# TensorE's order in the attention stage: values one head pair later, half blocks turned first

## The chip, the cores and the metric

The kernel runs on one core of a Trainium2 chip. The metric is the device time of one execution in microseconds (us). TensorE multiplies matrices and turns blocks, VectorE, ScalarE and GpSimd do the elementwise work, SyncE's queue starts most transfers. The core has SBUF as working memory and PSUM, eight banks of 128 x 512 fp32, as the place to which TensorE writes.

## The reference: causal attention, then a routed expert layer

```python
def _attn_ref(q, k, v):                      # batch 4, 12 heads, 448 tokens, head size 64
    scores = scale * np.matmul(q, k.transpose(0, 1, 3, 2))
    scores = np.where(mask, -1000000000.0, scores)      # mask: above the diagonal
    scores = scores - np.max(scores, axis=-1, keepdims=True)
    attn = np.exp(scores)
    attn = attn / (np.sum(attn, axis=-1, keepdims=True) + 1e-09)
    return np.matmul(attn, v)

def _moe_ref(x, w_gate, w1, w2):             # 1792 tokens of 768, 8 experts of 1024
    cap = N // E
    logits = x @ w_gate
    # all (token, expert) pairs in falling order of logit; a token goes to the first
    # expert that still has room for it (cap tokens each)
    ...
    for e in range(E):
        mask = assigned == e
        out[mask] = np.maximum(x[mask] @ w1[e], 0.0) @ w2[e]
```

The attention's output, heads side by side, is the `x` of the expert layer. Everything is fp32.

## The kernel before: a planned list of work for each engine

The 48 heads are taken as 24 head pairs (`NP`), six pairs to a batch. For one pair, with its two heads as sides 0 and 1, the attention stage does this.

- **Scores** (`scores`, L225): query blocks of 128 tokens against the keys that the causal mask leaves, blocks of 192, 320, 448 and 64 keys (`QM`). Two steps of two blocks each, (2, 3) and then (1, 0). The operands use 64 of the array's rows, one half for each side. The results go to PSUM tiles `s`, four buffers.
- **Masks** on VectorE (`mask`, L237): the mask is added, the maximum taken, the result lies in `Sm`. **Exponentials** on ScalarE (`exp`, L247) write the block of probabilities `P` (tile name `P`, two buffers) and the row sums `rs`.
- **Transposes** (`transp`, L257): 16 blocks of 128 x 128 are turned into PSUM tiles `t`, in four groups of four. Groups 0 and 1 are the whole blocks of side 0 and 1, group 2 more whole blocks of both sides, group 3 the half blocks of both sides.
- **Copies** of the turned groups (`keep_pt`, L280) into one of two tiles `PT`: group 0 and 1 on ScalarE (128 x 512 each), group 2 and the two halves of group 3 (64 x 256 each, numbers 3 and 4) on ScalarE or VectorE.
- **Values** (`av`, L292): `V` against `PT`, accumulated in one tile `t`; side 0 fills the array's first 64 columns, side 1 the others. The key block 0 comes first and needs the copies 0, 1, 3 and 4, the blocks 1 to 3 need copy 2. The result is copied to `xt` (L306), on ScalarE or VectorE.
- **Rows** (`rows_at`, L527; pairs 0 to 11 only): `xt` is turned back (L324) into a tile `t`, and VectorE divides by the row sums while it copies (L348). Pairs 12 to 23 are turned later, while the routing runs.
- **Logits** (`logits`, L542, and `logits_back`, L559): for sets of four pairs, `xt` against the gate weights (L359), a copy `lt`, four transposes (L378) and VectorE's sums (L398 to L407). The last two pairs go another way (L368).

All tiles `t` take turns in four PSUM buffers, in the order in which TensorE's steps are written out, so a step waits until the tile that stands four before its own has been read.

The order of the work comes from two places. TensorE's steps form one chain: `pe` (L454) makes every step depend on the step before, so TensorE does them as `plan` (L414) lists them, in its loop over `n`. The work of the other engines is put in order by `Schedule.run` (L123) before the kernel is built: it knows a duration for each task (the numbers in `add` calls), takes the earliest engine that has ready work, and there the task of the highest priority. The priority falls with the number of the pair (`pr = 5.5 - 0.1 * pp`), copies get 0.3 more, masks 0.25. The result is a fixed order of instructions for each engine; on the chip each engine works through its own, and semaphores do the waiting.

After attention come the routing rounds (class `Router`) and eight experts (class `Experts`), whose weights are loaded as the routing names each expert. They have a plan of their own that begins when attention ends.

Of the kernel before, what the change touches and what calls it, by code (L numbers as in the profile page):

```python
# [74 lines left out]
class Schedule:  # L75
# [7 lines left out]
    def add(self, eng, dur, fn, deps=(), prio=5.0, lat=None, delay=0.0, mode=0):  # L83
        t = Task(eng, dur, fn, prio, lat, delay, mode)
        for d in deps:
            if d is None:
                continue
            if d.end is None:
                d.users.append(t)
                t.wait += 1  # L90
            else:
                self.after(t, d)
        if not t.wait:
            self.put(t)
        return t
# [65 lines left out]
class Attention(Schedule):  # L161
# [252 lines left out]
    def plan(self, rt):  # L414
        add = self.add
        self.rings = {}
        self.got, self.gotv, self.vfree, self.qfree = {}, {}, {}, {}
        self.exps, self.pts, self.rec, self.xts, self.log, self.done_x = {}, {}, {}, {}, {}, []
        self.line = self.last_ev = None
        got, gotv = self.got, self.gotv  # L420
        prev = None
        for g in range(NP // 2):
            free = []
            if g >= 4:
                free = [self.event(0.0) for _ in range(2)]
                self.qfree[2 * g - 7], self.vfree[2 * g - 7] = free
            if g == 0:
                self.half0 = add("DMA", 0.7, self.load0, [], 9.5, 3.4)
            for p0, w in ((0, 1), (1, 1)) if g == 0 else ((2 * g, 2),):
                prev = add("DMA", 1.1 * w, lambda p0=p0, w=w: self.load(p0, w), [prev] + free, 9.0, 2.2 if prev else 3.8)  # L430
                for u in range(w):
                    got[p0 + u] = prev
            prev = gotv[g] = add("DMA", 1.1, lambda g=g: self.load_v(g), [prev] + free, 9.0, 2.2)
        for n in range(NP + 3):
            for lst in ((2, 3), (1, 0)):
                self.score_set(n, lst)
            self.turns(n - 1)
            self.rows_at(n - 3)
            self.logits_back(n - 3)
            self.values(n - 1)  # L440
            self.logits(n - 2)
        more = self.extras(rt)
        prev = None
        b3 = [self.log[b] for b in range(B - 1)]
        for n, early in more:
            prev = add("DVE", 0.3, n, [prev or self.exps[1, 1, 1]] + (b3 if early else []), 2.0)
        self.run()
# [36 lines left out]
    def turns(self, pp):  # L484
        if not 0 <= pp < NP:
            return
        pr = 5.5 - 0.1 * pp
        every = [(sd, i) for sd in range(2) for i in range(NC)]
        for g, need in ((0, [(0, 0), (0, 1), (0, 2)]), (1, [(1, 0), (1, 1), (1, 2)]), (3, every),
                        (2, [(0, 1), (0, 2), (1, 1), (1, 2)])):  # L490
            a = self.pe(0.44, lambda g=g: self.transp(pp, g), [self.exps[pp, sd, i] for sd, i in need] + self.ring("t", 4))
            last = [a]
            for c in (3, 4) if g == 3 else (g,):
                dur = {"DVE": 0.61, "ACT": 0.49} if c < 3 else {"DVE": 0.35, "ACT": 0.27}
                one = c < 2
                last = [self.add("ACT" if one else "ACT/DVE", dur["ACT"] if one else dur,
                                 lambda e="ACT", c=c: self.keep_pt(e, pp, c), last + self.ring("av", 2), pr + 0.3)]
                self.pts[pp, c] = last[0]
            self.rings.setdefault("t", []).append(last)

# [832 lines left out]
```

## Time and profile before

| | |
|---|---|
| median of 3 runs | 503.51 us (502.6 to 508.95) |
| profiled execution | 505.04 us, span of its instructions 503.3 us |
| attention stage in the profile | 0 to about 183 us, 24 head pairs |
| busy in the span | TensorE 487.1, its weight loads 409.2, VectorE 383.5, ScalarE 298.3, GpSimd 53.2 us |
| clock that TensorE was granted | 1.00 of full speed in the windows of the attention stage |

The span runs from the first instruction to the last of one execution; the time of the execution lies 1.74 us above it. Times of rows are counted from the start of the span. In the rows, PE is TensorE's matmuls, PEld its weight loads (which run ahead beside matmuls), DVE is VectorE, ACT ScalarE, POOL GpSimd. A row `t<-PT,v` is an instruction that writes tile `t` from `PT` and `v`. TensorE's fp32 matmuls appear as two records each, so a step of eight matmuls shows sixteen.

### The profile page before, as it was taken

The page shows a single profiled execution, that of the slowest core. Times are in us where ns is not written, and L with a number is a line of the kernel's source. Part 1 is how long each engine was busy: PE and PEld are TensorE (multiplying, and loading weights), DVE is VectorE, ACT ScalarE, POOL GpSimd, SP SyncE. Part 2 cuts the span into 40 slices and gives each one's busy share as a digit, 9 for nine tenths or more (in the row PEclk, how much of TensorE's full clock was granted, in tenths as well). Part 3 has the DMA queues.
Part 4 walks back from the last instruction along what each step waited for, and adds up shares of the span by engine and source line. Part 5 has one row for each costly group of instructions (what it writes and reads, how often), then busy time and mean ns, then how long its engine had stood idle before and what let it go on. Part 6 is the DMA issues. An engine that isn't in the chain of part 4 may idle for free.

```text
span 503.3 us, 10215 instructions
## 1 busy us (share of the span) xinstructions
PE 487.1 (97%) x3697; PEld 409.2 (81%) x3697; DVE 383.5 (76%) x1326; ACT 298.3 (59%) x749; POOL 53.2 (11%) x100
## 2 busy tenths in 40 slices
PE   8999999999999999899999999999999999999995
PEld 4676767766665676799998999989989999999994
DVE  4778878886776976589999999999999686594410
ACT  4887768777776853235655556645364574664410
POOL 6000000000000011010130120110022310210101
PEclk9999999999999999999999999999999999999999
DMA  8633183135000007748856876783793986682101
GB/s 280 265 109 112 44 294 120 43 115 191 37 0 1 3 31 238 267 158 327 257 185 188 295 221 211 223 265 124 234 314 99 322 278 229 190 288 73 56 1 55
DMA packets 19187, 84.84 MB, mean 169 GB/s; under 512 B 2240, under 2 KB 4928, under 8 KB 19136
## 3 DMA queue, kind: packets, MB, share of 16 engines
q1 hardware_dynamic: 16464, 73.14, 43.4%
q0 software_dynamic: 2672, 11.04, 6.9%
q8 instruction: 29, 0.48, 0.4%
q14 instruction: 22, 0.18, 0.1%
HBM read 73.16 MB, written 11.01 MB: 167 GB/s over the span
## 4 chain that ended last, share of the span: by engine, by line
PE 67%; DVE 16%; ACT 8%; DMA 5%; issue 3%; POOL 0%; POOLq 0%; DVEq 0%; ACTq 0%
PE po L1258 18%; PE t L297 11%; PE ph L1224 9%; PE s L233 8%; DVE wl L1154 5%; PE t L268 5%; PE ph L1228 4%; ACT P L254 4%; DMA xio<-xd,idx 4%; ACT PT L272 3%; PE ph L1219 3%; DVE G L697 2%; PE rt L798 1%; DVE Sm L244 1%; PE po L1219 1%
## 5 line engine op out<-in xcount | busy, mean ns | idle before, releaser
L1154 DVE TENSOR_TENSOR wl<-wr,wh 128x512 fp32r<-128x512 f32 x180 | 116.3, 685 | 14.2 <-ACT wh L1148 13.9
L1148 ACT CAST wh<-wr 128x1536 fp32r<-128x1536 f32 x60 | 88.9, 1481 | 60.7 <-DMA wr<-in_w 41.2
L254 ACT ACTIVATE P<-Sm,mx 128x448 f32<-128x448 f32 (+2 forms) x192 | 95.8, 500 | 39.7 <-DVE mx L244 39.3
L1224 PE MATMUL ph<-xhl,wh 128*128 128x448 f32 x336 | 109.2, 380 | 0.0
L1228 PE MATMUL ph<-xhl,wl 128*128 128x224 f32 x336 | 88.8, 264 | 0.0
L1258 PE MATMUL po<-wh,HH 128*112 128x384 f32 x256 | 68.2, 342 | 0.0
L1258 PE MATMUL po<-wh,HL 128*112 128x384 f32 x256 | 67.9, 341 | 0.0
L1258 PE MATMUL po<-wl,HH 128*112 128x384 f32 x256 | 67.3, 339 | 0.0
L1224 PEld LDWEIGHTS ph<-xhl,wh 128*128 128x128 f32 x336 | 63.1, 188 | 5.1 <-issue 0.6
L297 PE MATMUL t<-PT,v 128*64 128x192 f32 (+3 forms) x384 | 62.7, 387 | 3.4 <-ACT PT L272 2.5
L1228 PEld LDWEIGHTS ph<-xhl,wl 128*128 128x128 f32 x336 | 64.1, 191 | 0.0
L297 PEld LDWEIGHTS t<-PT,v 128*64 128x64 f32 x384 | 36.4, 136 | 31.1 <-ACT PT L272 15.8
L233 PE MATMUL s<-raw 64*128 64x448 f32 (+3 forms) x384 | 52.2, 406 | 0.3 <-DVE mx L244 0.2
L233 PEld LDWEIGHTS s<-raw 64*128 64x128 f32 x384 | 31.9, 188 | 19.4 <-issue 13.3
L268 PE MATMUL t<-idf,P 128*128 128x128 f32 x384 | 47.4, 276 | 0.0
L268 PEld LDWEIGHTS t<-idf,P 128*128 128x128 f32 x384 | 41.5, 140 | 6.1 <-issue 5.2
L1258 PEld LDWEIGHTS po<-wl,HH 128*112 128x112 f32 x256 | 44.0, 174 | 0.3
L1258 PEld LDWEIGHTS po<-wh,HL 128*112 128x112 f32 x256 | 43.2, 175 | 0.2
L1258 PEld LDWEIGHTS po<-wh,HH 128*112 128x112 f32 x256 | 43.1, 175 | 0.3
L244 DVE CUSTOM_DVE_ANT_0 Sm<-s,MK 128x448 f32<-128x448 f32 (+2 forms) x72 | 33.5, 486 | 11.3 <-PE s L233 10.8
L244 DVE CUSTOM_DVE_ANT_0 Sm<-s,MR 128x64 f32<-128x64 f32 (+3 forms) x120 | 40.1, 379 | 0.1
L1234 ACT ACTIVATE HH<-hs 128x224 fp32r<-128x224 f32 x56 | 21.9, 391 | 26.3 <-DVE hs L1242 24.5
(170 smaller groups left out, 625.8 us busy)
## 6 DMA issues: line engine op xcount, KB each, us to landing
wr<-in_w SPq DMA_DIRECT2D x64, 768.0 KB, 5.5
raw<-in_qk SPq DMA_DIRECT2D x11, 896.0 KB, 8.7
v<-in_v SPq DMA_DIRECT2D x12, 512.0 KB, 3.7
xd<-xio SPq DMA_DIRECT2D x2, 1152.0 KB
xd<-xio SPq DMA_DIRECT2D x3, 576.0 KB, 3.6
xd<-xio SPq DMA_DIRECT2D x3, 192.0 KB, 3.2
raw<-in_qk SPq DMA_DIRECT2D x1, 448.0 KB, 4.3
xd<-xio SPq DMA_DIRECT2D x1, 384.0 KB, 3.9
```

What stands on the lines that cost most here:

```text
L233: self.nc.tensor.matmul(ts[sd][:, o:o + m], q[:, 0, QS[i]:QS[i] + P], k, start=True, stop=True)
L244: self.nc.vector.tensor_tensor_reduce(Sm[:, QO[i] + sd * m:QO[i] + sd * m + m], self.S.pop((pp, sd, i)), mk, -0.125, 3.0e38, OP.add, OP.mi ...
L254: self.nc.scalar.activation(X[:, s], Sm[:, s], AF.Exp, bias=mx[:, sd, i:i + 1], scale=-1.0, accum_out=self.RS[b][:, pr, sd * NC + i:sd * N ...
L268: self.nc.tensor.transpose(t[:, n * P:n * P + P], X[:, o:o + P], idf)
L297: self.nc.tensor.matmul(self.AV[pp][sd * 64:sd * 64 + 64, XO[j]:XO[j] + KM[j]], self.V[2 * pp + sd][:, j, :], self.PTs[pp % 2][:, sd, KO[j ...
L1148: self.nc.scalar.copy(hi, self.R[p, c])
L1154: self.nc.vector.tensor_sub(lo[:, s], self.R[p, c][:, s], hi[:, s].bitcast(F32))
L1219: nc.tensor.matmul(t[:, c], self.R[p, f // 2][:, s], self.X[0, 0][:, d, 0, c], start=d == 0, stop=d == 5)
L1224: nc.tensor.matmul(t[:, :2 * CAP], hi[:, s], x[:, d].rearrange("p z t -> p (z t)"), start=d == 0, stop=False)
L1228: nc.tensor.matmul(t[:, :CAP], lo[:, s], x[:, d, 0], start=False, stop=d == 5)
L1234: self.nc.scalar.activation(self.HH[p][:, f], self.P[p, f][:, :CAP], AF.Relu)
L1258: self.nc.tensor.matmul(self.T[p, "o", u][z][:, :384], a[p][:, f, u * C:u * C + C], w[:, o:o + 384], start=f == 0 and n == 0, stop=f == 7 ...
```

## The change

In the loop of `plan` the call for values moves from behind the logits' transposes to ahead of the pair's transposes, and takes the pair before. For turn `n` TensorE's order was: scores of pair n, transposes of n-1, rows of n-3, logits' transposes, values of n-1, logits. It becomes: scores of n, values of n-2, transposes of n-1, rows of n-3, logits' transposes, logits.

In `turns` group 3, the half blocks, becomes the first of the four groups, ahead of 0, 1 and 2. Every group now waits for all eight exponentials of its pair; before, groups 0 and 1 waited for three of their own side, group 2 for four. The copies of group 3's two halves get 0.6 more priority instead of 0.3.

```diff
         for n in range(NP + 3):
             for lst in ((2, 3), (1, 0)):
                 self.score_set(n, lst)
+            self.values(n - 2)
             self.turns(n - 1)
             self.rows_at(n - 3)
             self.logits_back(n - 3)
-            self.values(n - 1)
             self.logits(n - 2)
...
-        for g, need in ((0, [(0, 0), (0, 1), (0, 2)]), (1, [(1, 0), (1, 1), (1, 2)]), (3, every),
-                        (2, [(0, 1), (0, 2), (1, 1), (1, 2)])):
+        for g, need in ((3, every), (0, every), (1, every), (2, every)):
...
+                up = 0.6 if c > 2 else 0.3
                 last = [self.add("ACT" if one else "ACT/DVE", dur["ACT"] if one else dur,
-                                 lambda e="ACT", c=c: self.keep_pt(e, pp, c), last + self.ring("av", 2), pr + 0.3)]
+                                 lambda e="ACT", c=c: self.keep_pt(e, pp, c), last + self.ring("av", 2), pr + up)]
```

## Rows read from the trace of the kernel before

**Rows 1.** The page: busy shares; costliest groups (busy, mean ns, idle before, releaser).
```profile
PE 487.1 (97%) x3697; PEld 409.2 (81%) x3697; DVE 383.5 (76%) x1326; ACT 298.3 (59%) x749; POOL 53.2 (11%) x100
...
L297 PEld LDWEIGHTS t<-PT,v 128*64 128x64 f32 x384 | 36.4, 136 | 31.1 <-ACT PT L272 15.8
```

**Rows 2.** Windows: length, then busy of PE, PEld, DVE, ACT, POOL.
```profile
20.00:30.00 10.00, 9.79 (x77) 7.32 (x76) 8.47 (x42) 9.43 (x33) 0.00 (x0) 1.00 0.48 159
...
51.18:80.55 29.37, 29.00 (x223) 20.21 (x222) 23.48 (x94) 22.30 (x77) 0.30 (x2) 1.00 0.42 146
...
139.31:168.67 29.36, 28.46 (x207) 18.98 (x206) 21.64 (x94) 22.41 (x78) 0.00 (x0) 1.00 0.00 1
```

**Rows 3.** Chain of waits, turns with rows: start us, us, engine, tile, line.
```profile
23.25 2.04 PE s L233 x16
...
27.62 2.31 PE t L297 x14
...
58.30 2.04 PE s L233 x16
60.34 1.90 PE t L268 x16
62.24 0.44 PE t L324 x4
62.67 2.75 PE t L297 x13
```

**Rows 4.** Chain of waits, a turn without rows.
```profile
146.43 1.17 PE s L233 x8
...
149.43 1.07 ACT PT L272 x2
...
151.60 1.94 PE t L297 x11
153.55 1.17 PE s L233 x8
```

**Rows 5.** Timeline, one turn: start us, us, engine, line, operation [idle before, releaser].
```profile
59.45 0.62 DVE L244 CUSTOM_DVE_ANT_0 Sm<-s,MK 128x448 f32<-128x448 f32 x1 [0.16 <-PE s L233]
...
61.24 0.35 DVE L244 CUSTOM_DVE_ANT_0 Sm<-s,MK 128x192 f32<-128x192 f32 x1
61.30 1.07 ACT L272 COPY PT<-t 128x512 f32<-128x512 f32 x2
...
62.26 0.68 ACT L254 ACTIVATE P<-Sm,mx 128x448 f32<-128x448 f32 x1
62.60 0.19 PEld L297 LDWEIGHTS t<-PT,v 128*64 128x64 f32 x2 [0.17 <-ACT PT L272]
...
63.05 0.37 ACT L272 COPY PT<-t 64x256 f32<-64x256 f32 x1
...
63.47 1.81 PEld L297 LDWEIGHTS t<-PT,v 128*64 128x64 f32 x14 [0.68 <-ACT PT L272]
...
65.45 0.62 DVE L274 COPY xt<-t 128x448 f32<-128x448 f32 x1 [1.21 <-PE t L297]
```

**Rows 6.** Chain of waits: a logits step, and the end of the attention stage.
```profile
72.53 0.89 PE t L359 x8
...
168.67 2.04 PE s L233 x16
...
172.72 2.69 PE t L297 x13
175.41 0.88 PE t L359 x4
176.29 1.90 PE t L268 x16
...
178.57 2.08 PE t L297 x14
```

**Rows 7.** Chain of waits: values of pair 1, ahead of scores of pair 3.
```profile
20.87 2.38 PE t L297 x14
```

## The prediction

> **What bounds the kernel now.** The first view is the page's busy shares [rows 1]: TensorE is busy for 97% of the span. That reading would leave nothing to win, so the second view asks how true it is by stage. In the attention stage TensorE counts 29.00 of 29.37 us as busy, its weight loads only 20.21, and VectorE and ScalarE 22 to 23 [rows 2]: no engine is plainly full. The Trainium skill, "Perfetto Trace Analysis", section Identifying the Most-Contended Engine, says that a tensor engine's matmul busy share is no measure of its limit and that the share of weight loads is a better one. The trace agrees (97% against 81%), and by the matmul share alone the sum below would be zero.
>
> The third view is the chain of waits. From 52 us on, a turn with rows reads: scores 2.04, transposes of the pair 1.90, row transposes 0.44, values 2.75 [rows 3], each behind the last, so TensorE's own order is the chain. But values needs only 1.94 once its operands are there [rows 4]. The missing 0.81 is seen in the fourth view, the timeline [rows 5]: of the 16 weight loads of a values step two start at 62.60 and fourteen at 63.47, after 0.68 us of waiting for ScalarE's copy of a half block into PT. That copy could not start before 63.05, because ScalarE had first done two whole-block copies (61.30, 1.07 us) and an exponential (62.26, 0.68 us) that stood ahead of it. Values of pair n comes straight after the transposes of pair n, with only 0.44 us of other work between, so the five copies are exposed on TensorE. In the second half, where no row transposes stand between, the chain leaves TensorE for ScalarE's copies on its way from scores to values, and a turn takes 7.12 us (153.55 minus 146.43) [rows 4] for 2.04 + 1.90 + 1.94 = 5.88 us of matmul work.
>
> **The change, step by step.** The program's order on TensorE is strict (each step depends on the one before), so the new order will be there.
>
> Step 1, values of a pair moved one turn later. Between scores of pair 3 (23.25) and scores of pair 23 (168.67) lie 20 turns and 145.42 us [rows 3, 6]. Their matmul work, from pieces of the chain that wait for nothing: 20 x (2.04 + 1.90 + 1.94) = 117.6; row transposes in 12 turns x 0.44 = 5.3; five logits steps x 0.89 = 4.5; five times their four transposes, as long as the rows', x 0.44 = 2.2 [rows 3, 4, 6]. Together 129.5, so 15.9 us (0.80 a turn) is waiting for copies. After the change, row transposes or nothing, then the scores of the next pair (2.04 us) stand between the last transpose and values. A turn with rows, counted from its scores: scores to 2.04, values to 4.0, transposes to 5.9, rows to 6.3, values of the turned pair at 8.4. The copies (two of 0.53, one of about 0.6, two halves of about 0.4) have 2.5 us against the 1.2 that they need now. I remove the whole 15.9.
>
> Step 2, what is late next. PSUM tiles t rotate over four buffers. The new order in them is values, group 3, 0, 1, 2, rows. Counted back four, group 2 takes the buffer of values of the same turn, so it waits for that tile's eviction. Three groups (12 transposes of about 0.11, some 1.4 us) cover VectorE's 0.62 us copy and its start [rows 5]. That leaves about 0.5 us, and a mask of 0.62 us in progress eats it. Likewise the row step waits for the two half-block copies, which is why being turned first helps them. ScalarE has 5.6 us of work a pair and VectorE 5.4 to 5.9 (two windows of four pairs each [rows 2]) against turns of 5.9 to 6.7: 85 to 95% full, in program order, so some waits will come back. Bounds: 0 a turn (scores and transposes in the chain of rows 3 lose nothing today) and 0.37 (what values loses in the early turns, 2.31 minus 1.94, with ScalarE 94% busy [rows 2, 3]). I take 0.15, nearer the lower end since only group 2's wait has a cover under one VectorE instruction: 20 x 0.15 = +3.
>
> Step 3, transposes all wait for every exponential of their pair. Group 3 is first and needs them all. Transposes of a pair now start 1.94 us later after the scores of the next pair than before, so this wait has more cover, not less. Zero; it would cost up to the last two exponentials, about 0.9, if ScalarE fell behind by more than 1.9 us.
>
> Step 4, changes of array shape. A turn has three before and three after, but scores to values, values to transposes and transposes to scores are new. Nearest rows: the narrow logits step costs 0.88 ahead of transposes and 0.89 ahead of scores, and transposes behind it take the usual 1.90 [rows 6]. The first weight load of values is idle for 0.17 behind the row transposes [rows 5], the only such gap that a row gives. Three new switches at up to 0.17 make 0.5; I take zero, with half of that, 0.25 a turn (5 us), either way as the bound.
>
> Step 5, both ends. In front, scores of pair 3 stand ahead of values of pair 1 instead of behind them: up to 2.4 us earlier [rows 7], or nothing if ScalarE's exponentials hold the transposes. At the back one values step (1.94) more follows the last scores, less the 0.75 that values of pair 22 waits now (2.69 minus 1.94) [rows 6], which the logits step then mostly covers. Net -1, bounds -3 and +2. Loads, row stores and routing constants: loads of v are freed a turn later, which is covered by their being issued seven pairs ahead; no queue is passed otherwise. The routing work of VectorE that starts after pair 19's logits keeps its order, and everything behind the last values (from 180.6 us) follows attention's end.
>
> Sum: -15.9 + 3 - 1 = -13.9 us. The profiled execution took 505.04 (span 503.3), so 491.1; it lies 1.5 above the median, 503.51, which gives 489.6. I forecast **490**, 2.7% less.
>
> **Rivals.**
> A second case, *the queues of ScalarE and VectorE bind*: the early turns show it, 6.68 us a turn with ScalarE at 9.43 of 10 [rows 2, 3]. All 20 turns at that pace would be 12 x 6.68 + 8 x 6.24 + 6.7 for logits = 136.8, so 8.6 saved and 1 at the ends: 494. Against it: in those turns values still stood right behind its copies. Chance 0.19.
>
> A third, *the copies stay late*: ScalarE does them behind all exponentials of the next pair. From a turn's start the first scores are there at 1.2 [rows 4] and the first mask at 1.9; the exponentials, ScalarE's 5.6 us less 1.4 of copies [rows 2, 5], take 4.2 and would end near 6.1 if nothing held them and near 7.6 as paced today, and copies behind them near 9.0, against the 8.4 at which values wants them: 0.6 lost a turn instead of 0.8, so 500 to 503. The Trainium skill, "PSUM — Partial Sum Buffer", section Engine vs sequencer instructions, calls ScalarE's queue a strict FIFO; the trace agrees, with the half copy at 63.05 behind the exponential of 62.26. Against this rival: copies of the older pair are given the higher priority, and the whole-block ones go promptly today. Chance 0.07.
>
> On the other side, *the eviction of values holds up group 2*. Today VectorE is idle for 1.21 us when values ends, and copies at once [rows 5]. In the new order values ends while masks of the newest pair run. If the copy stands behind a whole run of them (six from 59.45 to 61.59, 2.15 us [rows 5]), group 2 is late by 2.15 - 0.5 = 1.65 a turn, 33 us, and against the 16.9 saved that is 520, slower. It decides from 1.85 us of queueing a turn. Against it: the older pair's copy has the higher priority, so it should stand behind one mask. Chance 0.06.
>
> **How the numbers follow.** My case has 0.68: 485 to 493.4 with the bounds of steps 2, 4 and 5, its low end being all waits gone (503.5 - 15.9 - 3 = 484.6). Two per cent, about what a measurement of this kernel tells from no change, is 10 us, so 493.4. Faster: 0.68 and a little of the second case, 0.70. Within 2%: the rest of the second and the third, 0.24. Slower: 0.06. The range 484.5 to 500 takes in my case and the second, about 0.86.
>
> **What would show it.** Right: chain turns near 6.3 to 6.5 us with rows and 5.9 to 6.1 without; values at 1.94 to 2.0 with its weight loads started together; the idle time of its weight loads behind ScalarE's copies (15.8 us now [rows 1]) near zero; the last values ending near 167 instead of 180.7 us [rows 6]; the rest the same length. Wrong: the last four transposes of a pair waiting for the copy of values (the last rival), values waiting for PT as now (the third), scores or transposes longer than 2.04 and 1.90 without a wait (step 4), or the routing stage giving the gain back.

## The result, and the profile after

The median fell from 503.08 us (502.6 to 508.95, four runs; the forecast stood on the first three, 503.51) to **487.88 us** (485.98 to 492.33, four runs): a ratio of 0.9681, interval 0.9595 to 0.9766. The forecast was 490. The profiled execution took 486.56 us, its span 484.9, so the span is 18.4 us shorter than before. All of that lies in the attention stage of the two profiles. The last values step ends at 162.10 us instead of 180.66 [rows 6], 18.56 us earlier, and what follows it takes 322.8 us, against 322.64 before (503.3 minus 180.66).

The page first, busy shares and then the group of values' weight loads, which answers to [rows 1]:

```profile
PE 471.2 (97%) x3697; PEld 398.3 (82%) x3697; DVE 376.7 (78%) x1316; ACT 298.9 (62%) x759; POOL 52.6 (11%) x100
...
L297 PEld LDWEIGHTS t<-PT,v 128*64 128x64 f32 x384 | 25.4, 136 | 23.8 <-issue 14.0
```

TensorE's share is 97% as before, so this row alone would show no change. The second does: most of the idle time ahead of values' weight loads now ends with "issue" (14.0 of 23.8 us), where the engine waits for nothing that the profile shows. ScalarE's copies, 15.8 us of it before, no longer lead the list. Two windows of four pairs each, with the columns of [rows 2], show it by stage:

```profile
52.57:78.91 26.34, 26.34 (x223) 18.69 (x222) 22.05 (x94) 22.81 (x79) 0.30 (x2) 1.00 0.46 161
117.33:141.92 24.59, 24.59 (x206) 16.93 (x206) 20.42 (x88) 22.44 (x79) 0.00 (x0) 1.00 0.02 5
```

The same instructions of TensorE as in [rows 2] (223 matmul records in the first window) took 29.37 us and take 26.34, with no idle time left in either window. The chain of waits, a turn with rows, one without, and the end of the stage:

```profile
52.57 2.04 PE s L233 x16
54.61 1.88 PE t L297 x16
56.49 1.90 PE t L268 x16
58.39 0.44 PE t L324 x4
58.82 2.04 PE s L233 x16
...
129.40 2.04 PE s L233 x16
131.44 1.88 PE t L297 x16
133.32 1.90 PE t L268 x16
135.21 2.04 PE s L233 x16
...
148.17 2.04 PE s L233 x16
...
160.20 1.90 PE t L297 x16
```

From 25.35 us on the chain lies on TensorE alone. A turn with rows is 6.25 us (58.82 minus 52.57), one without 5.81 (135.21 minus 129.40), against 7.12 for both kinds before [rows 3, 4]. Values is 1.88 with all sixteen records in one piece; before, in the turns with rows from 52 us on, it was 2.75 with its weight loads split [rows 3, 5].

### The profile page after: what moved, and what is told of

It is laid out like the page before. It is cut to its first block, busy times and chain, and to the rows that moved or that the text cites. A ratio compares the mean times of both kernels' runs of the same rounds, so it can differ in the third digit from the quotient of the medians.

```text
span 484.9 us, 10216 instructions
## 1 busy us (share of the span) xinstructions
PE 471.2 (97%) x3697; PEld 398.3 (82%) x3697; DVE 376.7 (78%) x1316; ACT 298.9 (62%) x759; POOL 52.6 (11%) x100
## 4 chain that ended last, share of the span: by engine, by line
PE 77%; DVE 11%; ACT 5%; DMA 4%; issue 2%; POOL 1%; POOLq 0%; DVEq 0%; ACTq 0%
PE po L1258 23%; PE ph L1224 10%; PE s L233 9%; PE t L297 9%; PE t L268 8%; PE ph L1228 5%; DVE wl L1154 4%; PE ph L1219 3%; ACT P L254 3%; DMA xio<-xd,idx 2%; DVE G L697 2%; PE ph L1189 2%; PE rt L798 2%; DMA out<-xio,idx 1%; PE po L1219 1%
## 5 line engine op out<-in xcount | busy, mean ns | idle before, releaser
L297 PE MATMUL t<-PT,v 128*64 128x448 f32 (+3 forms) x384 | 46.8, 386 | 0.0
L297 PEld LDWEIGHTS t<-PT,v 128*64 128x64 f32 x384 | 25.4, 136 | 23.8 <-issue 14.0
L274 DVE COPY PT<-t 64x256 f32<-64x256 f32 (+1 forms) x56 | 29.6, 529 | 16.3 <-PE t L268 10.5
```

The lines of the kernel that those rows point to most:

```text
L274: self.nc.vector.tensor_copy(out, x)
L297: self.nc.tensor.matmul(self.AV[pp][sd * 64:sd * 64 + 64, XO[j]:XO[j] + KM[j]], self.V[2 * pp + sd][:, j, :], self.PTs[pp % 2][:, sd, KO[j ...
```

## The experiments

Each ratio is against runs of the kernel before on the same chip. An experiment is the kernel before or the changed kernel with one edit; the diff shows the edit, and `...` stands for lines left out.

### The order alone, the half blocks not first, as before

The changed kernel, with the groups in the order of before, 0, 1, 3, 2, and the old priority of the copies.

```diff
-        for g, need in ((3, every), (0, every), (1, every), (2, every)):
+        for g, need in ((0, [(0, 0), (0, 1), (0, 2)]), (1, [(1, 0), (1, 1), (1, 2)]), (3, every),
+                        (2, [(0, 1), (0, 2), (1, 1), (1, 2)])):
...
-                up = 0.6 if c > 2 else 0.3
```

> The new order of TensorE's steps with the groups of transposes as before (0, 1, 3, 2, each waiting for its own exponentials). Theory D (the turn by which values moved is the whole gain): the same as the changed kernel, 485 to 490 us, and values' weight loads wait for no copy of ScalarE. Rival H (the half blocks turned first bring part of it): the half copies come later again, 0.2 to 0.4 us lost in each of 20 turns, 491 to 496 us.

Measured: 489.07 us, ratio 0.9676 [0.9635, 0.9718]. The chain of waits:

```profile
53.54 2.04 PE s L233 x16
55.58 1.88 PE t L297 x16
57.46 1.90 PE t L268 x16
59.35 0.50 PE t L324 x4
59.86 2.04 PE s L233 x16
```

The turn is 6.32 us and the last values ends at 163.37, which is 1.27 us behind the full change. The order of TensorE's steps carries the whole gain as far as the times can tell: the two ratios are 0.0005 apart.

### The half blocks first alone, in the order of before

The kernel before, with group 3 first and the new priority of its copies.

```diff
-        for g, need in ((0, [(0, 0), (0, 1), (0, 2)]), (1, [(1, 0), (1, 1), (1, 2)]), (3, every),
-                        (2, [(0, 1), (0, 2), (1, 1), (1, 2)])):
+        for g, need in ((3, every), (0, every), (1, every), (2, every)):
...
+                up = 0.6 if c > 2 else 0.3
```

> The old order of TensorE's steps with the half blocks turned first. Theory D: the half copies get ahead of the exponential, but the copies of the whole blocks, 1.07 us of ScalarE, still stand between the last transposes and values: about half of the 0.8 us a turn stays, 494 to 499 us. Rival H: most of the gain, 486 to 491 us.

Measured: 507.96 us, ratio 1.0035 [1.0000, 1.0071]; the last values ends at 182.66, later than before. Both theories expected a gain, and there is none. The weight loads of values still wait for ScalarE's copies (14.2 us, 40 times). The chain of one turn:

```profile
111.19 1.17 PE s L233 x8
112.36 0.60 DVE Sm L244
...
113.07 1.75 ACT P L254 x6
...
114.84 0.37 ACT PT L272
...
115.24 0.59 ACT PT L272
...
115.87 2.43 PE t L297 x14
118.31 1.17 PE s L233 x8
```

The last copy to come is now that of a whole block (0.59 us) instead of a half block, and the turn is 7.12 us as before. So which copy comes last is not the point. The chain shows a **loop**, work that runs from one engine to the next and back to its start: the first half of the newest scores, its mask, the first exponentials of that pair, and only then, in ScalarE's fixed order, the older pair's remaining copies; then values, and behind values the next scores. The chain of [rows 4] has the same start and end. In these turns values waits for the copies that ScalarE does after those exponentials, and the next scores wait for values.

### Four more transposes ahead of values, in the kernel before and in the one after

Both kernels write four identity transposes into the tile that values then overwrites, 24 times. This is extra work on TensorE and nothing else.

```diff
             self.AV[pp] = self.ps.tile([P, 512], F32, name="t", bufs=4)
+            for i in range(4):
+                self.nc.tensor.transpose(self.AV[pp][:, i * P:i * P + P], self.k["idf"], self.k["idf"])
```

> The kernel before with four more transposes (of the identity, into the tile that values then overwrites) ahead of each values step: 24 x 0.44 = 10.5 us more work of TensorE, waiting for no copy. Theory D: values is waiting in that time anyway, so 503 to 506 us. Rival F (the values step is long for a reason on TensorE itself, and its whole share is work): 513 us or more.

> The changed kernel with the same four more transposes ahead of each values step. Theory D: TensorE has no waiting left in which to hide them, so all of it shows, 10.5 us and up to 3.5 more for an array shape that now changes four times a turn: 497 to 502 us. Rival Q (VectorE or ScalarE now set the pace and TensorE has slack): less than 5 us more, under 493 us.

Measured: on the kernel before 509.69 us, ratio 1.0086 [1.0053, 1.0119], between the 503 to 506 of theory D and the 513 of its rival; on the kernel after 499.41, ratio 0.9895 [0.9863, 0.9927], which is 0.0214 above the change, or 10.8 us. The chains of the kernel before with the extra work, and of the kernel after with it:

```profile
118.35 2.04 PE s L233 x16
120.39 1.90 PE t L268 x16
122.28 0.44 PE t L296 x4
122.72 2.75 PE t L299 x13
125.47 2.04 PE s L233 x16
```

```profile
56.07 2.04 PE s L233 x16
58.10 0.59 PE t L296 x4
58.69 1.88 PE t L299 x16
60.57 1.90 PE t L268 x16
62.47 0.44 PE t L326 x4
62.91 2.04 PE s L233 x16
```

In the kernel before the turn stays 7.12 us with 0.44 us more in it: the extra work sits in the wait. The first turns show the same, 6.68 us with the extra work (36.13 minus 29.45 in that profile's chain) and without it (36.61 minus 29.93), although the loop is shorter there. The last values ends only 1.68 us later, at 182.34, for 10.6 us of added work. The two profiled executions differ by 5.3 us (510.34 and 505.04). The rest of that lies behind the attention stage (326.3 us against 322.64), where nothing was changed; over the profiles of this document in which that part is the same code it takes from 321.9 to 326.35 us. In the kernel after every turn pays in full: 6.84 instead of 6.25 us, and the last values ends at 175.90, 13.8 us later (24 x 0.575). TensorE had no slack left. The time shows less than the profile, 10.8 us by the ratios, and the profiled execution was the slowest of the five (501.51).

This is also where a rule and the trace part. In the window from 52.57 us of the changed kernel, weight loads fill 18.69 of 26.34 us, 71%. The Trainium skill, "Perfetto Trace Analysis", section Identifying the Most-Contended Engine, would judge TensorE's headroom by that share, and by the share of its peak arithmetic that the kernel uses, rather than by its matmuls' 100%. Before the change the share of weight loads was 69% (20.21 of 29.37 us [rows 2]) and there was room indeed, although about 10% and not 31%. After it the share is nearly the same, and added work found no room. So here the matmul share tells whether more work fits into this order of steps, and the share of weight loads does not.

### The eviction of values behind the other work

This builds the rival on the other side: the copy of values' tile gets less priority than everything of the newer pair that stands in its way.

```diff
-        self.xts[pp] = self.add("ACT/DVE", {"ACT": 0.475, "DVE": 0.56}, ev, [a, self.xts.get(pp - 1)], pr + 0.3)
+        self.xts[pp] = self.add("ACT/DVE", {"ACT": 0.475, "DVE": 0.56}, ev, [a, self.xts.get(pp - 1)], pr - 0.6)
```

> The changed kernel with the copy of values' result (xt) at a lower priority, so that it stands behind all masks of the newest pair in VectorE's order. Theory E (the prediction's last rival, made on purpose: group 2 of the transposes waits for that copy and has about 0.5 us of cover): the copy starts some 0.4 to 1.0 us after values ends, 0.3 to 0.8 lost a turn, 493 to 504 us. Rival: the cover is ample, 486 to 490 us.

Measured: 493.52 us, ratio 0.9788 [0.9769, 0.9808], so 5.4 us of the gain are lost by the ratios. The edit moved more than a place in the order: in this trace 22 of the 23 whole copies of values run on VectorE, where the changed kernel has 4 there and 19 on ScalarE. The 5.4 us are the price of both together. Waits of the transposes' weight loads, from 20 to 170 us, and then the timeline around one of them (start, us, engine, line, operation, idle before and releaser):

```profile
PEld t L268 <- ACT PT L272: 5.7, 8, 1.2
```

```profile
80.43 1.04 ACT L272 COPY PT<-t 128x512 f32<-128x512 f32 x2
...
80.93 0.62 DVE L274 COPY xt<-t 128x448 f32<-128x448 f32 x1
...
81.05 0.66 PE L268 MATMUL t<-idf,P 128*128 128x128 f32 x4 [0.49 <-ACT PT L272]
```

The cost was in the range expected (493 to 504), the mechanism was not as expected. The last four transposes start at 81.05, before values' copy ends at 81.55 (80.93 + 0.62). They start as the first of ScalarE's two copies ends, about 80.95 (80.43 plus half of 1.04). So they did not take the buffer of values; by the time, they took that of group 0 of the same pair, whose copy stands behind the newest pair's exponentials. My text ahead of the result, four tiles counted back, does not hold at this place. The buffers are fixed when the program is built, so this is a fact of the program and not of the chip; no run shows how they were given out.

### Values one turn late, but behind the transposes

```diff
-            self.values(n - 2)
             self.turns(n - 1)
+            self.values(n - 2)
```

> The changed kernel with values of the older pair behind the transposes instead of ahead of them (scores n, transposes n-1, values n-2, rows). Theory D (only the turn's delay counts, not the place in the turn): 486 to 491 us. Rival P (the place counts: transposes come 1.9 us earlier and now wait for exponentials): 0.3 or more lost a turn, over 494 us.

Measured: 496.42 us, ratio 0.9833 [0.9805, 0.9860]. The time was in the range of the rival theory, but mostly not for its reason. Waits of weight loads from 20 to 170 us:

```profile
PEld t L297 <- ACT PT L272: 5.4, 17, 0.4
...
PEld t L268 <- ACT P L254: 0.9, 2, 0.7
```

The transposes hardly wait for exponentials. Values' weight loads do wait, although their own operands were copied a turn earlier. The timeline of ScalarE's copies in one turn, and the chain of the next, whose values step reads them:

```profile
58.28 1.47 ACT L272 COPY PT<-t 64x256 f32<-64x256 f32 x3
```

```profile
61.24 1.17 PE s L233 x8
...
63.12 1.75 ACT P L254 x6
...
64.89 0.38 ACT PT L272
...
65.31 1.95 PE t L297 x16
67.26 0.59 PE t L324 x4
```

ScalarE had done its copies for this values step by 59.75 (58.28 + 1.47), and VectorE the last one by 59.49. Yet values starts at 65.31, right behind a copy of the *newer* pair (64.89 + 0.38). It reads nothing of that copy, so what it waits for should be a PSUM tile; this is inferred, as the trace does not name the buffers. Behind four transpose groups all four buffers `t` are taken, and here the first to be emptied waits for a copy that stands behind the exponentials again. The loop is half closed through the buffers.

This wait is not the whole loss, and not every wait of a weight load delays TensorE. From scores of pair 3 (20.67) to scores of pair 23 (156.29) the stage takes 135.6 us, 6.9 more than with the change. By the starts in the timeline, values that begin late make about 3.3 us of this. A row step takes 0.59 us behind values and 0.44 behind transposes, 1.8 us in twelve turns. The five logits steps take about 2.1 us more, now that they stand close behind the values whose copy they read. Values ahead of the transposes, as the change has it, is therefore worth having, 7.7 us by the ratios, but the wait for buffers is only about half of the reason.

### ScalarE's order alone

TensorE's order is that of before; ScalarE must do the copies 0, 1, 3 and 4 of a pair ahead of the next pair's exponentials.

```diff
                 self.pts[pp, c] = last[0]
+                for sd, i in every if c != 2 and pp + 1 < NP else ():
+                    last[0].users.append(self.exps[pp + 1, sd, i])
+                    self.exps[pp + 1, sd, i].wait += 1
```

> The kernel before, in its old order on TensorE, with ScalarE's and VectorE's order planned so that the exponentials of the next pair come behind the copies of a pair's turned blocks 0, 1, 3 and 4. Theory L (a loop: scores, masks, exponentials, copies, values, scores; no order of ScalarE alone opens it, since copies 2.0 and exponentials 4.0 then stand in line between one pair's transposes and the next, 6.9 a turn): 497 to 503 us. Rival O (the whole loss was a bad order of ScalarE's queue): 486 to 493 us.

Measured: 498.05 us, ratio 0.9873 [0.9837, 0.9909]. The last values ends at 170.45, so the attention stage gained 10.2 us; 326.35 us behind it took part of that back. The chain, a turn without rows:

```profile
109.57 2.04 PE s L233 x16
111.61 0.60 PE t L268 x4
...
112.29 0.40 ACT PT L272
...
113.26 0.37 ACT PT L272
...
113.67 2.41 PE t L297 x14
116.08 2.04 PE s L233 x16
```

The turn is 6.51 us. The exponentials are out of the chain, so the loop through them is shown to be what made 7.12. The time is in the range of theory L, but that theory had said 6.9 a turn and that no order of ScalarE would open the loop. A turn with rows takes 6.51 too (61.89 minus 55.38 in the same profile's chain), so a shorter loop is left: values still stands 1.9 us behind the start of its transposes, and the copies themselves are exposed. Reordering ScalarE's queue takes the exponentials out of the loop; of the versions tried, only moving values puts other matmuls over the copies.

### A further step: more row transposes in the turns

The rows of six more pairs, 18 instead of 12, are turned in the attention stage. That loads the full TensorE there and leaves six pairs for the routing, in two pieces fewer.

```diff
-LATE = 12
-PIECES = {14: 3, 17: 3, 20: 3, 22: 2, 23: 1}
+LATE = 18
+PIECES = {20: 3, 22: 2, 23: 1}
```

> The changed kernel with the rows of 18 pairs instead of 12 turned in the attention stage (the rest in the routing stage as before). Theory D (TensorE is full in attention and has no hiding place left): 6 x 0.44 = 2.6 us more there; in the routing stage VectorE and ScalarE lose twelve half row blocks, of which VectorE's cost 0.33 us each in line: 483 to 488 us. Rival: the routing stage does not shorten, 489 to 492 us.

Measured: 488.03 us, ratio 0.9697 [0.9623, 0.9770], not to be told from the change. The last values ends at 165.66, 3.56 us later, where 6 x 0.44 = 2.6 was expected, and the rest takes 321.1 us, 1.7 less. That difference is within what this part varies by from profile to profile. No version tried is measurably faster than the change.

## Why the prediction was right, step by step

**Step 1** (−15.9) held. From scores of pair 3 to scores of pair 23 (148.17) I count the timeline's starts: 19.36 and 148.10 against 23.18 and 168.60 before, so 128.7 us instead of 145.4. The forecast of bare matmul work was 129.5. All 15.9 us went, and 0.8 more: values at 1.88 instead of 1.94 gives 1.2 (20 x 0.06), and some 0.5 went to two row steps that still waited (25.35 and 31.83, 0.66 us each instead of 0.44, and a gap ahead of the first).

**Step 2** (+3) was mis-sized: those two row steps, some 0.5 us, are all that came back, and they are counted in step 1's 16.7. In the waits of weight loads from 20 to 163 us (waited for, us in all, times, longest):

```profile
PEld t L297 <- ACT P L254: 1.4, 6, 0.2
...
PEld t L268 <- ACT P L254: 0.2, 1, 0.2
```

The transposes wait 0.2 us in the whole stage, and values is not seen to wait for a copy into PT. One other wait of a values step is longer, 0.7 us once. A reason that the rows show is where the eviction went: at 56.54 ScalarE copies `xt` (0.53 us), right behind values, ahead of the copies into PT. It does so for 19 of the 23 whole copies.

```profile
56.54 0.53 ACT L272 COPY xt<-t 128x448 f32<-128x448 f32 x1
...
57.94 1.04 ACT L272 COPY PT<-t 128x512 f32<-128x512 f32 x2
```

I had put it on VectorE, where it stood before [rows 5], among masks. That ScalarE and VectorE are 84 to 87% full (22.81 and 22.05 of 26.34 us) cost nothing that the chain shows.

**Step 3** (0) held, by the transposes' 0.2 us above. **Step 4** (0, either way up to 5) held: scores 2.04, transposes 1.90, values 1.88, none longer than before at the new neighbours.

**Step 5** (−1, bounds −3 and +2) measured −1.9: in front scores of pair 3 come 3.82 us earlier (23.18 minus 19.36; I had at most 2.4), and behind scores of pair 23 the stage takes 13.93 us (162.10 minus 148.17) against 11.99 [rows 6], 1.94 more. By the timelines' starts, 2.31 of the front's gain are values of pair 1, which left that stretch; 0.70 that values of pair 0 takes less (16.66 minus 14.08 before, 17.47 minus 15.59 after), 0.55 an earlier start of the scores of pair 1 (9.07 instead of 9.62), and 0.26 the steps between. I had counted only the first of these. The 0.55 is not due to the change. Those scores also started at 9.08 us with the half blocks first in the order of before, and at 9.14 in the kernel before with four more transposes, but at 9.90 with the new order alone.

The sum: −16.7, 0 and −1.9 make −18.6, where I had −13.9; the profiles differ by 18.4 in the span and by 18.48 in the time. The medians are only 15.2 us apart. The profiled run of before lay above its median and that of after below its own, and the two runs of after above its median were granted a lower clock on the mean: 489.2 at 0.993 and 492.33 at 0.986, against 485.98 at 0.997 and 486.56 at 0.999. So 490 stood close to the median partly by luck: the +3 of step 2, which was not there, offset that spread. The signs that I had named show it too. They came out beyond the forecast: turns of 6.25 and 5.81 us (I had 6.3 to 6.5 and 5.9 to 6.1), values at 1.88 (1.94 to 2.0), and its last step ending at 162.1 (167).

**The rivals.** Bound queues (494) did not come: turns of 6.25, not 6.68. The late copies (500 to 503) did not come either, since values' weight loads were not seen to wait for copies any more. The eviction rival (520) needs a late copy to bite; the experiment that made it late cost 5.4 us and not 33, as the group of transposes did not wait for that buffer where it was looked at.

**What my reading missed.** I had named the five exposed copies as the cause. The rows held a plainer sign: turns with and without row transposes both took 7.12 us [rows 3, 4], although one has 0.44 us more TensorE work. A turn whose length doesn't follow TensorE's work is paced by something else, here by a loop from scores through mask and exponentials to ScalarE's copies and values. The runs bear it out: 0.44 us more work left 7.12, another last copy left 7.12, ScalarE's order alone gave 6.51, and taking values out of the loop gave the bare matmul time. The loop has no one length: in the first turns of the kernel before it was 6.68 [rows 3]. In the one from 29.93 to 36.61 us VectorE did both half-block copies, and from 52 us on ScalarE did the last of them; no run tests whether that is the whole difference.

## What to carry to other kernels

Where a turn keeps its length though its work differs, look for a loop that runs through another engine's queue, and test it by adding work to the engine that looks full: work that costs nothing there means a wait. To break such a loop, let the consumer use operands made a turn earlier, and try it ahead of the step that takes the shared buffers. Here the eviction of its result had then to be prompt, while the order of the copied groups made no difference that the times could tell.

## What the runs showed of the hardware that was not expected

- Four transposes cost 0.44 us behind other transposes and 0.59 between scores and values: 0.15 us more, where they split two steps of other array shapes. The pair's sixteen transposes hold about the same once, 1.90 us against four times 0.44, behind scores before the change and behind values after it. Scores to values showed no such gap (2.04 and 1.88).
- The share of weight loads in the attention windows went only from 69% to 71% while TensorE's slack there, three of 29.4 us in four turns, went to nothing.

Left open: what the half blocks' order is worth by itself, as its 1.27 us at the end of the attention stage are below what the times can tell; how much of the late eviction's 5.4 us is lateness and how much VectorE's extra work; and by what rule the program's buffers were given out.
